# Bias rows of the last eleven groups kept in the transposed x: two heads stored at once, the rest two units later

## Chip, cores and metric

The kernel runs on one core of a Trainium2 chip. The metric is the device time of one execution in microseconds, the median of three runs. The profile is of one further execution of the same program.

## What is computed

Attention with a position bias that is computed on the way, followed by a gated feed-forward layer. Shapes: q, k, v are 4 x 8 x 576 x 64 (batch, heads, positions, width), the feed-forward weights 512 x 2048 and 2048 x 512.

```
psi  = log1p(|i - j|) / log1p(max(i, 1))          # 576 x 576, the same for all batches
bias = relu(psi * w1 + b1) @ w2                   # hidden 32, one value per head
attn = softmax(q k^T / 8 + bias) @ v
x    = attn with the heads side by side           # 2304 x 512
h    = x @ w_in
out  = (h * cos(h)) @ w_out
```

## The kernel before

Everything is float32; matmuls of the attention and the feed-forward layer use operands split in a high and a low float32r half. Work is put on the engines in the order in which the program issues it, and waits follow from reads and writes of the same bytes.

**First stage, the bias.** The 576 query positions are 36 groups of 16, put in five tiles: tile 4 has four groups, tiles 0 to 3 eight each. They are made in the order of `todo`: tile 4, then 0, 1, 2, 3. For a group DVE (one step in six: ACT) makes the hidden values `ht`, PE multiplies them with w2 into PSUM (`pa`, L356), and `bias_store` (L366) copies the 591 columns that the 16 positions share, scaled by the position's factor, into a buffer `rt` (L374, once on DVE, L372) and issues one store to `sc`, a DRAM tensor per tile (L375). Partition 8r + h of `rt` is head h of row r, so one store carries all eight heads: 128 rows. `ra` has eight `rt` buffers.

**Loads of the bias.** `load_bias(hp, t, heads)` (L267) reads the rows of tile t for the two heads of pair hp back from `sc` into `bt` tiles, each row shifted by one, so that every query position sees its own bias. For a head 0 that is one load, for a head 1 two (L273). The loads of the first pair are issued in the loop of the first stage, at steps n = 13 (tile 4), 20 and 21 (tile 0), 28 and 29 (tile 1), and after the last store (tiles 2 and 3). Those of later pairs follow in the last unit of the pair before.

**Attention.** There are 16 units (hp, b): four head pairs, and in each the four batches. A unit has five slots, one for each tile in the order 0, 1, 4, 2, 3; slot i is tile `tiles[i % 5]` of unit `i // 5`. In a slot PE makes the scores (`s`, L440) into two PSUM buffers, one for each head; DVE adds the bias and takes the maximum (L453); ACT takes the exponential (L471) and, on its other steps, copies turned blocks (`act_copy`, L529); GpSimd normalizes (L494). PE turns the result (L501) and multiplies with v (`pv`, L569) for slots that lie before. `keep_x` (L579) copies the product into `xT`, [128, 4, 2304]: its first quarter is written by units 0 to 3, the others by units 4 to 15.

**Loads in the slots.** Each slot ends with issues on SP's queue: v, k and q of later units (`load`, L153) and, in slots 5 and 6, the first two blocks of feed-forward weights (`load_w`, L77, tile `raw`). ACT reads the first of these in slot 9 (`abs_w`, L92), the second ten slots later. Loads, stores and bias loads all go through SP, which issues them in the program's order and stands while an instruction waits.

**Feed-forward.** It takes up the time behind some 280 us and runs on PE with both weight matrices.

Of the kernel before, what the change touches and what calls it, by code (L numbers as in the profile page):

```python
# [9 lines left out]
F32 = mybir.dt.float32  # L10
# [18 lines left out]
def kernel(  # L29
# [11 lines left out]
    nc = tc.nc  # L41
# [6 lines left out]
    RB = S + 15  # L48
    PITCH = S + 32
    GP = 16 * (8 * PITCH - 1)  # L50
# [15 lines left out]
    xT = const.tile([128, HP, NT], F32, name="xT")  # L66
    xs = const.tile([128, 2, KD, TB], F32R, name="xs")
    wpre = [const.tile([128, 2, 2, 512], F32R, name=f"wpre{i}") for i in range(WPRE)]
    sc = [dram.tile([1, (8 if t < 4 else 4) * GP + 16], F32, name=f"sc{t}") for t in range(5)]
# [7 lines left out]
    def load_w(fc, part):  # L77
        r = wk.tile([128, 512, 2], U32, tag="raw", name="raw")
        if part == 0:
            nc.sync.dma_start(  # L80
                out=r.rearrange("p (c x) y -> p c (x y)", c=KD),
                in_=w_in[:, fc * 256 : fc * 256 + 256].rearrange("(c p) x -> p c x", p=128),
            )
        else:
            nc.sync.dma_start(out=r.rearrange("p x y -> p (x y)"), in_=w_out[fc * 128 : fc * 128 + 128, :])
        raw[fc, part] = r
# [25 lines left out]
    with tc.manual_schedule():  # L112
        tail, front, stage = ExitStack(), ExitStack(), ExitStack()

        def opened(stack, name, bufs, side, space=None):
            kw = {} if space is None else {"space": space}
            return stack.enter_context(tc.tile_pool(name=name, bufs=bufs, side=side, reuse_waits="tile", **kw))
# [92 lines left out]
        def keep_hi(u, x, ps):  # L210
            for (hi, _), i, scale in halves_of(u, x, ps):
                nc.scalar.activation(out=hi, in_=i, func=AF.Copy, scale=scale)
# [8 lines left out]
        def bank(dt=F32):  # L221
            return ps_t.tile([128, 512], dt, tag="t", name="pt")
# [4 lines left out]
        def turn(u, x, ps):  # L227
            n = natural(u, x)
            for i, c in enumerate((4,) if x == "x" else range(4)):
                nc.tensor.transpose(ps[:, 128 * i : 128 * i + 128], n[:, c], ident)  # L230
            return ps
# [35 lines left out]
        def load_bias(hp, t, heads=range(2)):  # L267
            if t < 4:
                for h in heads:
                    bt = bp.tile([128, 576], F32, tag="b", name="bt")  # L270
                    src = sc[t]
                    for to, at, n in ((0, 0, S),) if h == 0 else ((0, 512, 64), (64, 0, 512)):
                        nc.sync.dma_start(  # L273
                            out=bt[:, to : to + n],
                            in_=bass.AP(
                                src.tensor,
                                src.offset + (2 * hp + h) * PITCH + 15 + at,
                                [[8 * PITCH - 1, 128], [1, n]],
                            ),
                        )  # L280
                    bias[hp, t, h] = bt
            else:
                bt = bp.tile([128, 576], F32, tag="b", name="bt")
                src = sc[t]
                for h in range(2):
                    nc.sync.dma_start(
                        out=bt[64 * h : 64 * h + 64],
                        in_=bass.AP(
                            src.tensor,
                            src.offset + (2 * hp + h) * PITCH + 15,  # L290
                            [[8 * PITCH - 1, 64], [1, S]],
                        ),
                    )
                bias[hp, t, 0] = bt

        ha = opened(stage, "ha", 10, "left")
        ra = opened(stage, "ra", 8, "left")
# [12 lines left out]
        wparts = [(fc, p) for fc in range(WPRE) for p in range(2)]  # L310
# [13 lines left out]
        for g in range(4):  # L324
            r = slice(32 * g, 32 * g + 32)
# [4 lines left out]
        def bias_hid(k):  # L330
            qi = groups[todo[k][0]][todo[k][1]]
            n = max(S - 16 * qi, 16 * qi + 16)
            hts = []
            for s in range(4):
                ht = ha.tile([128, S], F32, tag="h", name="ht")
                o = 4 * qi + s
                e = edge[:, o : o + 1]
                if s == 3 and k in ACT_H:
                    nc.scalar.activation(out=ht[:, 0:n], in_=wl[:, 0:n], func=AF.Relu, bias=e)  # L339
                else:  # L340
                    nc.vector.tensor_scalar(ht[:, 0:n], wl[:, 0:n], e, 0.0, ALU.add, ALU.max)  # L341
                hts.append(ht)
            return hts

        def bias_rows(k, hts):
            nr = 16 * groups[todo[k][0]][todo[k][1]] + 15
            ps = ps_a.tile([128, 1024], F32, tag="a", name="pa")
            at = 512 - nr if RB - 512 <= nr <= 512 else 0
            cuts = sorted({0, nr, 512 - at, RB})
            for a, b in zip(cuts, cuts[1:]):  # L350
                for s, ht in enumerate(hts):
                    if a < nr:
                        i = ht[:, nr - b + 1 : nr - a + 1][:, ::-1]
                    else:
                        i = ht[:, a - nr : b - nr]
                    nc.tensor.matmul(  # L356
                        ps[32 * s : 32 * s + 32, at + a : at + b],
                        nbd,
                        i,
                        start=True,  # L360
                        stop=True,
                        tile_position=(0, 32 * s),
                    )
            return ps[:, at : at + RB]

        def bias_store(k, ps):  # L366
            t, gi = todo[k]
            qi = groups[t][gi]
            rt = ra.tile([128, RB], F32, tag="r", name="rt")
            m = mrow[:, qi : qi + 1]  # L370
            if k == len(todo) - 2:
                nc.vector.tensor_scalar(rt, ps, m, None, ALU.mult)  # L372
            else:
                nc.scalar.activation(out=rt, in_=ps, func=AF.Copy, scale=m)  # L374
            nc.sync.dma_start(  # L375
                out=bass.AP(sc[t].tensor, sc[t].offset + gi * GP, [[PITCH, 128], [1, RB]]),
                in_=rt,
            )

        tiles = [0, 1, 4, 2, 3]  # L380
        for i in range(WPRE):
# [5 lines left out]
        todo = [(t, gi) for t in (4, 0, 1, 2, 3) for gi in range(len(groups[t]))]  # L387
        held, hts = None, bias_hid(0)
        nc.vector.tensor_copy(mrow, pm[:, 0:NQ])
        for n in range(len(todo) + 1):  # L390
            now = hts
            if n < len(todo):
                hts = bias_hid(n + 1) if n + 1 < len(todo) else None
                ps = bias_rows(n, now)
            if held:
                bias_store(*held)
            for t, heads in {13: ((4, ()),), 20: ((0, (0,)),), 21: ((0, (1,)),), 28: ((1, (0,)),), 29: ((1, (1,)),)}.get(n, ()):
                load_bias(0, t, heads)
            if n == len(todo):
                load_bias(0, 2)  # L400
                load(3, "k", (2, 3))
                load_bias(0, 3)
            held = (n, ps)
            if n in SECOND:
                load(2, *SECOND[n])
            if n in T_FIRST:
                halved[n] = turn(*T_FIRST[n], bank())
                keep_hi(*T_FIRST[n], halved[n])
            if n - 1 in T_FIRST:
                keep_lo(*T_FIRST[n - 1], halved[n - 1])  # L410
# [184 lines left out]
        W_MID = [(3, 9)]  # L595
        W_PLAN = [(0, 2), (0.5, 3), (1, 7), (2, 8), ("load", 8), (4, 12)]
        W_LATE = 10
        REST = {2: (1, 2), 3: (3, 4)}
        get = lambda i: jobs[i] if 0 <= i < len(jobs) else None

# [15 lines left out]
        def slot(i):  # L616
# [23 lines left out]
            else:  # L640
                if now:
                    qk(u, j)
                if last:
                    for h in heads_of(last):
                        softmax_exp(*last, h)
            weights(i - W_LATE, W_EARLY)
            if prev and prev[1] in (0, 2):
# [38 lines left out]
            if prev:  # L686
                keep_main(*prev, 0, pm[0])
            weights(i - W_LATE, W_MID)
            if j == 4 and u >= 1:
# [28 lines left out]
            if now:  # L718
                if i == 1:
                    load(0, "v")  # L720
                for du, x in LOAD_PLAN[j]:
                    if u + du < NU:
                        load(u + du, x, (0, 1) if (u, x) == (0, "k") else None)
                if i in (5, 6):
                    load_w(*wparts[i - 5])
                hp, b = units[u]
                if b == B - 1 and hp + 1 < HP:
                    load_bias(hp + 1, tiles[j])
                if i in X_EARLY:
                    split_x(0, 0, X_EARLY.index(i))  # L730
            weights(i - W_LATE, W_PLAN)
        for i in range(len(jobs)):
# [125 lines left out]
        def ffn_step(i, begun=False):  # L858
# [13 lines left out]
            if now:  # L872
                g, n, fc = now
                nx = steps[i + GF] if i + GF < len(steps) else None
                if nx:
                    for c in ((0, 1), (2, 3), (), ())[fc - g * GF]:
                        split_x(nx[0], nx[1], c)
                for step in REST.get(i, ()):
                    widen_w(*wparts[-1], step)
# [79 lines left out]
```

## Time and profile before

| | us |
|---|---|
| median of 3 runs | 695.43 |
| lowest and highest | 694.91, 697.91 |
| the profiled execution | 695.13 |
| its span, first to last instruction | 693.3 |
| PE busy | 679.7 (98%) |
| DVE busy | 580.8 (84%) |
| ACT busy | 435.8 (63%) |
| POOL busy | 398.2 (57%) |

PE, DVE, ACT and POOL are the engines for matmuls, for vectors, for activations, and GpSimd; PEld is PE's loading of weights, which runs beside its matmuls; SPq is the queue on which SP issues transfers. Times are from the start of the span. In the timeline an engine's idle time before an instruction stands in brackets, with what ended it. A line in the profile is a line of the kernel.

### The profile page before, as it was taken

To read this page: it belongs to the slowest core of one execution; us is meant where nothing else is said; L and a number is where in the kernel's file an instruction comes from. 1 tells how busy PE (TensorE), PEld (TensorE's weight loads), DVE (VectorE), ACT (ScalarE), POOL (GpSimd) and SP (SyncE) were. 2 spreads that over 40 slices of the span, in tenths; PEclk is the share of its full clock that TensorE was granted. 3 is DMA by queue.
4 is the path that set the end of the run, shared out by engine and by line. 5 is a ranking of instruction groups with operands and counts; after the bars stand their busy time and mean duration, and the time that the engine had idled before them with its cause. 6 is when DMAs were issued, how large, how long until landed. Compare 5 with 4: busy or idle time off the path is not lost.

```text
span 693.3 us, 15601 instructions
## 1 busy us (share of the span) xinstructions
PE 679.7 (98%) x5747; PEld 561.9 (81%) x5747; DVE 580.8 (84%) x1345; ACT 435.8 (63%) x938; POOL 398.2 (57%) x480
## 2 busy tenths in 40 slices
PE   6998999999999999999999999999999999999997
PEld 3666777777777777799989898998988888999986
DVE  8998888888888888678788789999899899876666
ACT  6998888988889887545565554454544544433342
POOL 0008888898988989646456356265374474463300
PEclk9999999999999999999999999999999999999999
DMA  6798546437337311012011111110111110011112
GB/s 161 266 350 224 130 122 168 104 85 220 71 92 200 99 50 41 10 31 61 30 34 60 30 49 44 32 61 32 34 58 31 57 35 32 0 46 46 47 46 92
DMA packets 84445, 58.57 MB, mean 84 GB/s; under 512 B 62224, under 2 KB 70800, under 8 KB 84368
## 3 DMA queue, kind: packets, MB, share of 16 engines
q1 hardware_dynamic: 83024, 56.88, 28.4%
q8 instruction: 46, 0.75, 0.5%
q10 hardware_dynamic: 1344, 0.69, 0.4%
q14 instruction: 31, 0.25, 0.1%
HBM read 41.94 MB, written 15.61 MB: 83 GB/s over the span
## 4 chain that ended last, share of the span: by engine, by line
PE 93%; DMA 3%; DVE 1%; POOL 1%; ACT 1%; issue 0%; SPq 0%; DVEq 0%; POOLq 0%
PE ph L759 29%; PE po L805 29%; PE pv L569 12%; PE s L440 11%; PE pm L501 6%; PE pa L356 4%; DMA sc<-rt 2%; PE pt L501 1%; PE spare L501 1%; DMA lt<-in_ltab_dram 1%; DMA bt<-sc 1%; POOL P L494 0%; DVE ht L341 0%; ACT ht L339 0%; DVE acc L829 0%
## 5 line engine op out<-in xcount | busy, mean ns | idle before, releaser
L453 DVE CUSTOM_DVE_ANT_0 P<-s,bt 128x576 f32<-128x576 f32 x144 | 103.8, 753 | 24.4 <-PE s L440 24.1
L494 POOL TENSOR_SCALAR P<-P,rc 128x576 f32<-128x576 f32 x144 | 108.3, 764 | 24.3 <-DVE rc L487 11.5
L763 ACT ACTIVATE a<-ph,quarter 128x384 int32<-128x384 f32 x96 | 55.7, 581 | 97.8 <-PE ph L759 96.9
L555 POOL TENSOR_TENSOR xs<-xT,xs 128x384 fp32r<-128x384 f32 x96 | 108.1, 1126 | 8.0
L471 ACT ACTIVATE P<-P,m 128x576 f32<-128x576 f32 x144 | 110.0, 768 | 0.6 <-DVE m L453 0.6
L759 PE MATMUL ph<-xs,wpre 128*128 128x384 f32 x576 | 109.4, 338 | 0.0
L759 PE MATMUL ph<-xs,w 128*128 128x384 f32 x576 | 108.5, 337 | 0.0
L774 ACT ACTIVATE r<-r,hpi 128x384 f32<-128x384 f32 x96 | 59.3, 617 | 74.8 <-DVE r L770 74.6
L759 PEld LDWEIGHTS ph<-xs,wpre 128*128 128x128 f32 x576 | 101.9, 188 | 5.4 <-DVE a L778 0.9
L759 PEld LDWEIGHTS ph<-xs,w 128*128 128x128 f32 x576 | 101.3, 188 | 5.1 <-DVE a L778 1.2
L769 DVE SCALAR_TENSOR_TENSOR r<-a,ph 128x384 f32<-128x384 int32 x96 | 52.8, 550 | 62.7 <-ACT a L763 62.6
L440 PE MATMUL s<-kN,qT 64*128 64x288 f32 (+1 forms) x864 | 92.0, 311 | 2.0 <-DVE m L453 1.4
L440 PEld LDWEIGHTS s<-kN,qT 64*128 64x128 f32 (+1 forms) x864 | 70.7, 185 | 27.2 <-DVE dn L484 7.6
L554 POOL TENSOR_SCALAR xs<-xT 128x384 fp32r<-128x384 f32 x96 | 63.2, 658 | 29.7 <-PE ph L759 29.7
L788 DVE TENSOR_TENSOR gl<-a,gh 128x384 fp32r<-128x384 f32 x96 | 75.8, 789 | 0.4 <-ACT gh L782 0.4
L569 PE MATMUL pv<-PT,vN 128*64 128x320 f32 (+1 forms) x512 | 76.0, 418 | 0.0
L805 PE MATMUL po<-wpre,gh 128*128 128x512 f32 x288 | 75.3, 397 | 0.0
L805 PE MATMUL po<-w,gh 128*128 128x512 f32 x288 | 75.2, 395 | 0.0
L110 POOL TENSOR_TENSOR w<-wb,w 128x512 fp32r<-128x512 f32 x16 | 20.8, 1297 | 87.6 <-ACT w L108 87.6
L782 ACT ACTIVATE gh<-a 128x384 fp32r<-128x384 f32 x96 | 49.8, 518 | 23.6 <-DVE a L778 23.6
L770 DVE SCALAR_TENSOR_TENSOR r<-a,r 128x384 f32<-128x384 int32 x96 | 61.0, 636 | 3.3
L805 PEld LDWEIGHTS po<-wpre,gh 128*128 128x128 f32 x288 | 53.4, 188 | 9.4 <-issue 0.5
(98 smaller groups left out, 1166.8 us busy)
## 6 DMA issues: line engine op xcount, KB each, us to landing
sc<-rt SPq DMA_DIRECT2D x36, 295.5 KB, 4.5
raw<-in_moe_w_in_dram SPq DMA_DIRECT2D x16, 512.0 KB, 3.7
raw<-in_moe_w_out_dram SPq DMA_DIRECT2D x16, 512.0 KB, 3.5
bt<-sc SPq DMA_DIRECT2D x16, 288.0 KB, 4.0
out_dram<-acc SPq DMA_DIRECT2D x17, 256.0 KB, 2.0
nk<-in_k_dram SPq DMA_DIRECT2D x32, 128.0 KB, 3.5
bt<-sc SPq DMA_DIRECT2D x16, 256.0 KB, 4.2
vN<-in_v_dram SPq DMA_DIRECT2D x32, 128.0 KB, 2.8
```

Of the source, the lines that this page charges most:

```text
L440: nc.tensor.matmul(s[h][:, hf, 0:HALF], qTs[u % 2][r, a, 128 * t : 128 * t + 128] if t < 4 else qTs[u % 2][:, a, 512:640], kN[u][r, b, o : ...
L453: nc.vector.tensor_tensor_reduce(neg.rearrange("p (a x) -> p a x", a=2), s[h][:, :, 0:HALF], bias[hp, t, h].rearrange("p (a x) -> p a x", ...
L471: nc.scalar.activation(out=P[u, j][:, 576 * h : 576 * h + 576], in_=neg, func=AF.Exp, bias=m[:, 0:1], scale=-1.0, accum_out=dn[u, j][:, h ...
L494: nc.gpsimd.tensor_scalar(p, p, r, 1.0, ALU.mult, ALU.mult)
L554: nc.gpsimd.tensor_scalar(h, src, 1.0, 1.0, ALU.mult, ALU.mult)
L555: nc.gpsimd.tensor_tensor(l, src, f(h), ALU.subtract)
L569: nc.tensor.matmul(ps[64 * h : 64 * h + 64, 0 : WQ[hf]], a, m, start=(c == 0), stop=(c == 4), tile_position=(0, 64 * h), skip_group_check= ...
L759: nc.tensor.matmul(ps, a, x, start=(i == 0), stop=(i == 3 * KD - 1))
L770: nc.vector.scalar_tensor_tensor(r, n, -TWO_PI_LO, r, ALU.mult, ALU.add)
L774: nc.scalar.activation(out=r, in_=r, func=AF.Sin, scale=SIN_SCALE, bias=hpi)
L788: nc.vector.tensor_tensor(gl, a, f(G[key][0]), ALU.subtract)
L805: nc.tensor.matmul(O[n][i], a[:, 128 * i : 128 * i + 128], w, start=(i0 == 0 and p == 0), stop=(i0 == GF - 1 and p == 2),)
```

## The change

The rows of the last eleven groups (three of tile 2, all of tile 3) are written into slices of `xT`, of which the last three quarters are free until unit 5 writes them, and no longer into a buffer of `ra`. At once only heads 0 and 1 of them are stored, with one store of 16 rows for each head. The full 128 rows are stored by `store_rows` in slots 6 to 14, and write heads 0 and 1 a second time with the same values. The bias of tile 2 for the first pair is loaded at steps n = 33 and 34 and no longer after the last store; there the two small loads of unit 3's k now come first and tile 3's bias follows. The first two weight blocks are loaded in slots 8 and 9 and no longer in slots 5 and 6.

```diff
+        rest = xT[:, 1:].rearrange("p h n -> p (h n)")
+        late = [rest[:, RB * i : RB * i + RB] for i in range(11)]
+
+        def store_rows(k, rt):
+            t, gi = todo[k]
+            nc.sync.dma_start(
+                out=bass.AP(sc[t].tensor, sc[t].offset + gi * GP, [[PITCH, 128], [1, RB]]),
+                in_=rt,
+            )
+
         def bias_store(k, ps):
             t, gi = todo[k]
             qi = groups[t][gi]
-            rt = ra.tile([128, RB], F32, tag="r", name="rt")
+            n = k - len(todo) + len(late)
+            rt = late[n] if n >= 0 else ra.tile([128, RB], F32, tag="r", name="rt")
             m = mrow[:, qi : qi + 1]
...
-            nc.sync.dma_start(
-                out=bass.AP(sc[t].tensor, sc[t].offset + gi * GP, [[PITCH, 128], [1, RB]]),
-                in_=rt,
-            )
+            if n < 0:
+                store_rows(k, rt)
+            else:
+                for h in range(2):
+                    nc.sync.dma_start(
+                        out=bass.AP(sc[t].tensor, sc[t].offset + gi * GP + h * PITCH, [[8 * PITCH, 16], [1, RB]]),
+                        in_=rt[h:128:8],
+                    )
...
-            for t, heads in {13: ((4, ()),), 20: ((0, (0,)),), 21: ((0, (1,)),), 28: ((1, (0,)),), 29: ((1, (1,)),)}.get(n, ()):
+            for t, heads in {13: ((4, ()),), 20: ((0, (0,)),), 21: ((0, (1,)),), 28: ((1, (0,)),), 29: ((1, (1,)),), 33: ((2, (0,)),), 34: ((2, (1,)),)}.get(n, ()):
                 load_bias(0, t, heads)
             if n == len(todo):
-                load_bias(0, 2)
                 load(3, "k", (2, 3))
                 load_bias(0, 3)
...
+        STORES = {6: (0, 1), 7: (2, 3), 10: (4, 5), 11: (6, 7), 12: (8,), 13: (9,), 14: (10,)}
...
-                if i in (5, 6):
-                    load_w(*wparts[i - 5])
+                if i in (8, 9):
+                    load_w(*wparts[i - 8])
+                for n in STORES.get(i, ()):
+                    store_rows(len(todo) - len(late) + n, late[n])
```

## Rows read from the trace of the kernel before

**Rows 1.** The page: busy time of PE and its share, instructions.
```profile
PE 679.7 (98%) x5747; PEld 561.9 (81%) x5747; DVE 580.8 (84%) x1345; ACT 435.8 (63%) x938; POOL 398.2 (57%) x480
```

**Rows 2.** Windows: length; busy PE, PEld, DVE, ACT, POOL; clock; DMA share; GB/s.
```profile
40.00:50.00 10.00, 10.00 (x153) 6.18 (x145) 9.88 (x27) 10.00 (x17) 0.00 (x0) 1.00 1.00 351
50.00:60.00 10.00, 8.41 (x101) 6.23 (x94) 6.87 (x21) 7.35 (x20) 5.69 (x8) 1.00 0.86 293
60.00:70.00 10.00, 8.86 (x121) 6.74 (x122) 8.65 (x33) 8.37 (x23) 9.71 (x14) 1.00 0.83 200
70.00:80.00 10.00, 10.00 (x136) 7.63 (x137) 7.67 (x26) 8.32 (x22) 8.82 (x13) 1.00 0.53 137
```

**Rows 3.** Waits from 36 to 75 us: total, times, longest.
```profile
PE s L440 <- DVE m L453: 1.4, 4, 0.7
...
DVE P L453 <- DMA bt<-sc: 0.3, 1, 0.3
```

**Rows 4.** Timeline around the first unit: start, length, instruction, idle time before.
```profile
51.21 0.76 ACT L374 ACTIVATE rt<-pa,mrow 128x591 f32<-128x591 f32 x1 [1.08 <-issue]
...
52.96 0.27 PE L230 MATMUL pt<-ident,nk 128*128 128x128 f32 x1
...
59.38 0.76 DVE L453 CUSTOM_DVE_ANT_0 P<-s,bt 128x576 f32<-128x576 f32 x1 [0.32 <-PE s L440]
...
61.87 0.76 DVE L453 CUSTOM_DVE_ANT_0 P<-s,bt 128x576 f32<-128x576 f32 x1 [0.31 <-PE s L440]
...
62.92 0.76 DVE L453 CUSTOM_DVE_ANT_0 P<-s,bt 128x576 f32<-128x576 f32 x1 [0.29 <-DMA bt<-sc]
...
63.75 1.05 PE L440 MATMUL s<-kN,qT 64*128 64x288 f32 x11 [0.66 <-DVE m L453]
```

**Rows 5.** The chain that ended last, from 36 to 75 us: start, length.
```profile
52.02 5.73 DMA sc<-rt
...
58.88 3.88 DMA bt<-sc
```

**Rows 6.** SP's queue: start, length, issues.
```profile
52.48 2.08 SPq L273 DMA_DIRECT2D bt<-sc  x3
...
57.82 1.50 SPq L273 DMA_DIRECT2D bt<-sc  x3
...
66.67 0.59 SPq L80 DMA_DIRECT2D raw<-in_moe_w_in_dram  x1
...
67.90 1.25 SPq L175 DMA_DIRECT2D nk<-in_k_dram  x2
...
70.53 1.73 SPq L175 DMA_DIRECT2D nq<-in_q_dram  x2
77.51 1.11 SPq L160 DMA_DIRECT2D vN<-in_v_dram  x2
```

**Rows 7.** Tile sc over the whole span: issue in ns, transfers from issue to landing.
```profile
L375 SPq DMA_DIRECT2D sc<-rt x36: 319/429/1752, 11.3 to 52.0; - x36
...
DMA to landing us min/median/max: 2.1/4.2/6.3
```

**Rows 8.** Tile raw from 60 to 130 us: issue to landing.
```profile
DMA to landing us min/median/max: 4.1/5.4/6.5
```

**Rows 9.** ACT's timeline in slot 9.
```profile
75.61 0.66 ACT L92 ACTIVATE wb<-raw 128x512 f32<-128x512 f32 x1
76.83 0.60 ACT L529 ACTIVATE PT<-pm 128x512 f32<-128x512 f32 x1 [0.56 <-PE pm L501]
78.09 0.44 ACT L529 ACTIVATE xT<-pv 128x320 f32<-128x320 f32 x1 [0.67 <-PE pv L569]
```

**Rows 10.** DVE by shape from 20 to 28 us: busy, mean ns.
```profile
L341 DVE TENSOR_SCALAR ht<-wl,edge 128x416 f32<-128x416 f32 x3 | 1.1, 428 | 0.0
```

**Rows 11.** The same from 36 to 44 us.
```profile
L341 DVE TENSOR_SCALAR ht<-wl,edge 128x416 f32<-128x416 f32 x4 | 1.5, 431 | 0.0
```

**Rows 12.** PE's timeline: the turn of the next k, slot 17.
```profile
97.83 0.41 PE L501 MATMUL spare<-ident,nk 64*128 64x64 f32 x8
```

## The prediction

> **What bounds the kernel now.** I read the engine totals first: PE is busy for nearly the whole span [rows 1]. What a change of loads and stores can win must therefore come out of PE's idle time. The windows say where that lies: PE loses 1.59 us between 50 and 60 us and 1.14 us between 60 and 70 us, 2.73 us together, and nothing in the stretch before or behind [rows 2]. The same rows show what tempts one to make this change: the DMA engines' share is 1.00 between 40 and 50 us, while the last bias rows are stored, and still 0.86 and 0.83 in the two windows after it.
>
> The second reading is who waits. Between 36 and 75 us one wait of a compute engine for a bias load is listed, 0.3 us long [rows 3]. The timeline shows it: DVE adds the second head of tile 3 at 62.92 us and has been idle for 0.29 us for that load; the first head of tile 3 and the first of tile 2 waited for PE's scores, not for a load [rows 4]. The chain names the transfers behind it: the last store of rows takes 5.73 us from its issue at 52.02 us, the load that waits for it leaves at 58.88 us and needs 3.88 us [rows 5]. So the store is on the chain that ended last, but only the last 0.29 us of it hold an engine up; the rest runs beside work that fills the time anyway. A share of the chain is not a saving.
>
> **The change part by part.** *Fewer bytes in the stores of groups 25 to 35.* A group is 128 rows of 591 floats, 302.6 kB; two heads of it are 32 rows, 75.6 kB. Eleven groups lose 11 x 227.0 = 2.50 MB, at the 351 GB/s of the window [rows 2] 7.1 us of DMA time before 52 us. The engines that make the rows do the same work into another buffer: PE, DVE and ACT have no idle time there to give back (10.00, 9.88 and 10.00 of 10 us, [rows 2]). Nor does the full DMA share lengthen their instructions: DVE's 416-column step takes 428 ns before the queue is full and 431 ns while it is [rows 10, 11]. This edit alone wins nothing; it only lets tile 3's rows land sooner.
>
> How much sooner: ACT writes the last group from 51.21 us for 0.76 us [rows 4], so its two stores leave at about 52.0 and 52.4 us (an issue takes 319 ns at least, 429 in the median, [rows 7]). Nearly idle, a transfer of this tensor lands in 2.1 us; in the full queue it takes up to 6.3 us [rows 7]. Both ends stay open. I take 2.1 to 3 us, since the eleven small stores bring a quarter of the bytes: landed at 54.5 to 55.4 us instead of 57.75. The loads of k that stand ahead of tile 3's bias in the queue need PE's turn at 52.96 us for 0.27 us [rows 4] and take about 1.25 us (two such issues, [rows 6]), so SP is free for the bias at 54.5 us at the earliest. Its three issues take 1.50 us [rows 6]; tile 3 leaves by 56.9 us and lands, with 3.9 us as before [rows 5], by 60.8 us, where DVE asks for it at 62.63 us (61.87 + 0.76, [rows 4]). Even at 5.73 us for the store it would be no later than before by more than one extra issue, 0.4 us.
>
> *What the vanished wait is worth.* DVE's second head starts at 62.63 instead of 62.92 us. PE stood for 0.66 us on the maximum that it gives [rows 4]; 0.37 us of that stay. Behind it PE is full from 70 us on [rows 2], so the 0.29 us can be carried to the end, if nothing there has less slack than PE. Bounds 0 and 0.29; I take 0.29.
>
> *Tile 2's bias loaded at steps 33 and 34.* Its issues go from 52.48 us, where they take 2.08 us of SP's time [rows 6], to some 3 us earlier. DVE needs tile 2 at 59.38 us and waits for PE there [rows 4]: worth nothing by itself, and it clears SP for tile 3, as counted. It puts a wait on SP for tile 2's last store, five groups back, and behind it queue the small stores of tile 3. These no longer hold a buffer of the ring of eight, so ACT doesn't wait for them.
>
> *Eleven full stores in slots 6 to 14.* They add 3.33 MB, 9.5 us of DMA time at 351 GB/s, from about 64 us on, where the share was 0.83 and then 0.53 [rows 2]. On SP each costs 0.32 to 0.66 us. Nobody waits for them until the second pair's bias loads. What they push back is the loads behind them. Those of slots 10 to 14 come behind the load of v at 77.51 us, which waits for PE [rows 6]; the next k and q are turned on PE only at 97.83 us [rows 12], so 2 to 3 us of extra issues before them are covered.
>
> *The first weight block, slot 8 instead of slot 5.* This is the edit that can cost. Before, it was issued at 66.67 us [rows 6] and ACT first reads it at 75.61 us [rows 9], with 4.1 us to landing at best and 6.5 at worst among the weight loads near [rows 8]: at least 2.4 us to spare. Now four full stores (1.3 to 2.6 us, 1.7 at the median issue), the k loads (67.90 to 70.53, 2.6 us) and the q loads (1.73 us) go ahead of it [rows 6, 7]: 6.0 us later, 72.7 us. Against that SP is past tile 3's bias at 56.4 us or so instead of 59.32 us (57.82 + 1.50, [rows 6]), 2.9 us sooner: 69.8 us. It lands between 73.9 and 76.3 us. ACT would ask 0.29 us sooner, at 75.3 us, so the middle has no wait. And ACT has 0.56 and 0.67 us of idle time in the same slot [rows 9], so a landing up to 76.5 us moves no copy that PE needs. I take 0.
>
> [...]
>
> Sum: 695.13 us of the profiled execution (693.3 of span, 1.83 around it) - 0.29 + 0 + 0 = 694.84 us. The median of the runs is 0.30 us above that execution: 695.1 us.
>
> **The rivals.** *The full queue was behind more of PE's idle time.* Then up to all 2.73 us come back: 692.7 us on the median. For it speaks that the gaps lie in the two windows with a DMA share of 0.86 and 0.83 [rows 2]; against it that only 0.3 us of waits name a load [rows 3], and that the heads before waited for scores [rows 4]. Those are the turns of two score buffers between PE and DVE, which no store touches. Chance 0.08.
>
> *The first weight block comes late (slower).* If SP wins nothing at tile 3 and the queue fills with the full stores, it is issued at 72.7 us and lands after 6.5 us at 79.2 us: 3.6 us after 75.61, less 1.23 us of ACT's slack, 2.4 us on PE: 697.5 us with the 0.29 us won. It decides from a landing at about 76.8 us on. For it: one slot between issue and use where there were four, and 605 kB of stores directly ahead of k and q; against it, 4.1 us is what a weight load took in a share of 0.83. With issues at 0.66 us and both mishaps it would reach 698.4 us. Chance 0.17.
>
> *The small stores cost as much of the queue as full ones (no change).* Then the last lands 5.73 us after an issue that comes one issue later; tile 3's wait stays and grows by up to 0.4 us: 695.4 to 695.9 us. For it: the count of stores in the stage doubles, and SP needed 0.43 us for each; against it, the two bounds of landing, 2.1 and 6.3 us [rows 7], differ with the load of the queue, and bytes fall to a quarter. Chance 0.13.
>
> **How the numbers follow.** The forecast has 0.62: 695.1 us, between 694.8 and 695.4 us by the bounds of its one term. The runs of before lie from 694.91 to 697.91 us, so half a per cent (3.5 us) is about what a measurement tells from no change. All four cases end inside it but for the tails. Range 693.0 to 697.6 us: it takes in the second rival's worked case and most of the first's. Faster by over 0.5% would take under 691.95 us, more than all of PE's idle time between 50 and 70 us: 0.03. Slower needs over 698.9 us, a weight block beyond 80 us or a wait not seen here: 0.06. Within: 0.91.
>
> **What would show it.** Right: the DMA share between 44 and 52 us well below 1, tile 3's bias issued near 55 us, no DVE wait for it, PE's wait near 63.5 us down to about 0.4 us, and everything behind earlier by some 0.3 us. The weight block issued near 70 us and ACT's first step on it with no idle time. Wrong: ACT idle for that block before about 75.3 us and PE idle soon after; a wait of the copies into the first quarter of xT (about 71, 78 and 85 us) for the stores that read its other quarters, if they are taken for one buffer; or PE's gaps between 52 and 62 us closing although no load was named in them.

## The result, and the profile after

The changed kernel takes 703.01 us (median of four runs, 701.71 to 704.88), the kernel before in the same comparison 695.54 us: ratio 1.0107, 95% interval 1.0091 to 1.0123. The forecast was 695.1 us with a range up to 697.6. The loss of 7.5 us is larger than any rival's.

The page of the changed kernel first. PE's busy time is 2 us longer than in [rows 1], the span 7.7 us.

```profile
PE 681.8 (97%) x5747; PEld 563.3 (80%) x5747; DVE 580.7 (83%) x1345; ACT 435.9 (62%) x938; POOL 396.7 (57%) x480
```

Its windows, columns as in [rows 2]. The DMA share between 40 and 50 us did fall, from 1.00 to 0.72. PE's busy time between 60 and 70 us fell too, from 8.86 to 4.00 us, and its clock column is 0.83 in two windows.

```profile
40.00:50.00 10.00, 10.00 (x152) 6.31 (x148) 10.00 (x29) 10.00 (x18) 0.00 (x0) 1.00 0.72 244
50.00:60.00 10.00, 8.46 (x98) 6.21 (x92) 6.89 (x22) 7.71 (x19) 4.91 (x7) 1.00 0.46 126
60.00:70.00 10.00, 4.00 (x56) 3.19 (x55) 4.56 (x15) 4.82 (x12) 5.42 (x8) 0.83 0.55 137
70.00:80.00 10.00, 10.00 (x125) 7.71 (x125) 7.20 (x26) 6.76 (x20) 7.57 (x10) 0.83 0.75 214
```

What VectorE (DVE) waited for, from its timeline in the changed kernel (start, length, idle time before and what ended it): three waits for bias loads, the second head of tile 2 and both of tile 3, 5.29 us together, where before there was one of 0.29 us [rows 4].

```profile
61.48 0.76 DVE L467 CUSTOM_DVE_ANT_0 P<-s,bt 128x576 f32<-128x576 f32 x1 [0.57 <-DMA bt<-sc]
...
66.71 0.76 DVE L467 CUSTOM_DVE_ANT_0 P<-s,bt 128x576 f32<-128x576 f32 x1 [3.73 <-DMA bt<-sc]
...
68.47 0.76 DVE L467 CUSTOM_DVE_ANT_0 P<-s,bt 128x576 f32<-128x576 f32 x1 [0.99 <-DMA bt<-sc]
```

And why the load was late: SP's queue in the changed kernel (start, length, issues). L390 is the store of one head, L273 the bias load. From 42.42 to 61.92 us SP issues 22 stores and six loads almost without a gap. Tile 3's bias leaves at 63.56 us, in the kernel before at 57.82 [rows 6].

```profile
42.42 4.40 SPq L390 DMA_DIRECT2D sc<-xT  x6
46.86 0.58 SPq L273 DMA_DIRECT2D bt<-sc  x1
47.54 1.73 SPq L390 DMA_DIRECT2D sc<-xT  x2
49.32 1.05 SPq L273 DMA_DIRECT2D bt<-sc  x2
50.47 4.91 SPq L390 DMA_DIRECT2D sc<-xT  x8
55.42 0.58 SPq L273 DMA_DIRECT2D bt<-sc  x1
56.10 1.10 SPq L390 DMA_DIRECT2D sc<-xT  x2
57.25 1.06 SPq L273 DMA_DIRECT2D bt<-sc  x2
58.41 3.51 SPq L390 DMA_DIRECT2D sc<-xT  x4
62.02 0.68 SPq L175 DMA_DIRECT2D nk<-in_q_dram  x1
62.74 0.64 SPq L175 DMA_DIRECT2D nk<-in_k_dram  x1
63.56 1.40 SPq L273 DMA_DIRECT2D bt<-sc  x3
```

ACT isn't what holds it up. It writes the first late group at 41.58 us and the last at 51.93 us, 0.72 us later than before [rows 4]. The last two stores leave only some 9 us after that. This is ACT's timeline:

```profile
41.58 0.81 ACT L385 ACTIVATE xT<-pa,mrow 128x591 f32<-128x591 f32 x1
...
51.93 0.76 ACT L385 ACTIVATE xT<-pa,mrow 128x591 f32<-128x591 f32 x1 [1.03 <-PE pa L356]
```

The view of the tensor sc in the changed kernel gives what one issue costs (min, median, max in ns). A store of 16 rows takes 587 ns of SP's time in the median, one of 128 rows out of the ring 406 ns: fewer rows don't make an issue shorter here.

```profile
L371 SPq DMA_DIRECT2D sc<-rt x25: 319/406/1534, 11.5 to 41.8; - x25
L390 SPq DMA_DIRECT2D sc<-xT x22: 472/587/1613, 42.4 to 61.3; - x22
```

So the rows of SP's queue add up: 15.65 us for the 22 stores, 3.27 us for the six loads and 0.58 us between the rows are 19.5 us, for eleven groups that ACT (for one of them DVE) writes in 11.1 us. Of the 15.65 us, 22 x 0.587 = 12.9 us are the stores at the median; the rest is gaps of SP and a few long issues, of which the first of the four at 58.41 us takes 1.61 us (the maximum in the row above). What makes these long isn't settled. A hint: beside this issue, between 56 and 60 us, and beside one of 1.10 us at 47.54 us, the transfers show one of 16 KB of the program's own instructions. The line from 56 to 60 us (packets, MB, share):

```profile
q8 instruction: 1, 0.02, 1.6%
```

The rest of the loss is put down to the clock. After the wait PE's granted clock is 0.50 until about 73.5 us, an estimate from the 0.65 between 72 and 74 us; windows of 2 us of the changed kernel show it:

```profile
64.00:66.00 2.00, 0.00 (x0) 0.00 (x0) 0.00 (x0) 0.53 (x1) 1.86 (x3) 1.00 0.71 170
66.00:68.00 2.00, 0.47 (x1) 0.28 (x1) 0.77 (x2) 0.49 (x1) 0.00 (x0) 0.65 0.99 252
68.00:70.00 2.00, 0.85 (x7) 0.71 (x8) 1.53 (x6) 1.11 (x4) 0.00 (x0) 0.50 0.66 148
70.00:72.00 2.00, 2.00 (x25) 1.88 (x25) 1.13 (x4) 0.47 (x4) 1.80 (x3) 0.50 0.95 214
72.00:74.00 2.00, 2.00 (x13) 1.01 (x15) 1.48 (x8) 1.95 (x8) 1.46 (x3) 0.65 0.69 205
74.00:76.00 2.00, 2.00 (x24) 1.22 (x20) 1.28 (x3) 0.85 (x3) 2.00 (x4) 1.00 0.92 272
```

PE's timeline of the changed kernel agrees: the eleven score matmuls behind the wait take 1.80 us, where [rows 4] has 1.05.

```profile
69.29 1.80 PE L454 MATMUL s<-kN,qT 64*128 64x288 f32 x11 [1.15 <-DVE m L467]
...
105.22 0.41 PE L515 MATMUL spare<-ident,nk 64*128 64x64 f32 x8
```

The last row is the turn of slot 17, at 97.83 us before [rows 12]: 7.39 us later. Of these 0.72 us were there at ACT's last group, from the first part of the stage, where nothing is changed (in the eleven profiled executions of the changed kernel and the experiments DVE's first score is taken between 52.2 and 53.4 us, in no order that goes with the edits); 5.29 - 0.29 = 5.00 us are DVE's waits; 1.67 us are left, and the lower clock is what the trace shows for them: the same 5747 matmuls keep PE busy for 2.1 us longer. This is a remainder and not a measurement of its own; the run with the wait filled, below, bears on it.

### The profile page after: what moved, and what is told of

It reads as the page before. It is cut to its first block, busy times and chain, and to the rows that moved or that the text cites. A ratio compares the mean times of both kernels' runs of the same rounds, so it can differ in the third digit from the quotient of the medians.

```text
span 701.0 us, 15611 instructions
## 1 busy us (share of the span) xinstructions
PE 681.8 (97%) x5747; PEld 563.3 (80%) x5747; DVE 580.7 (83%) x1345; ACT 435.9 (62%) x938; POOL 396.7 (57%) x480
## 4 chain that ended last, share of the span: by engine, by line
PE 93%; DVE 3%; DMA 1%; ACT 1%; SPq 1%; issue 1%; DVEq 0%; ACTq 0%
PE ph L776 29%; PE po L822 29%; PE pv L583 12%; PE s L454 11%; PE pm L515 6%; PE pa L356 4%; PE spare L515 1%; PE pt L515 1%; DVE ht L341 1%; DMA lt<-in_ltab_dram 1%; DVE P L467 1%; DMA bt<-sc 1%; SPq L390 0%; ACT ht L339 0%; ACT xT L385 0%
## 5 line engine op out<-in xcount | busy, mean ns | idle before, releaser
L822 PEld LDWEIGHTS po<-wpre,gh 128*128 128x128 f32 x288 | 53.4, 188 | 9.4 <-issue 0.5
```

What stands on the lines that cost most here:

```text
L822: nc.tensor.matmul(O[n][i], a[:, 128 * i : 128 * i + 128], w, start=(i0 == 0 and p == 0), stop=(i0 == GF - 1 and p == 2),)
```

## The experiments

Theory A: SP's queue can't issue two stores for each group in the time of a group, so the last rows leave late; bytes, order and the later stores don't matter. Theory B: the moved bias loads or the loads of k now ahead of tile 3's bias hold the queue. Theory C: the stores and weight blocks in the slots cost the time. Ratios are to the kernel before, with 95% intervals. Unless said, edits are to the changed kernel.

**One store for both heads.** The heads of a pair are put at places hp and hp + 4 of a row's eight (columns of w2 in another order), so that 32 rows, every fourth partition, hold the first pair.

```diff
-                for h in range(2):
-                    nc.sync.dma_start(
-                        out=bass.AP(sc[t].tensor, sc[t].offset + gi * GP + h * PITCH, [[8 * PITCH, 16], [1, RB]]),
-                        in_=rt[h:128:8],
-                    )
+                nc.sync.dma_start(
+                    out=bass.AP(sc[t].tensor, sc[t].offset + gi * GP, [[4 * PITCH, 32], [1, RB]]),
+                    in_=rt[0:128:4],
+                )
...
-                                src.offset + (2 * hp + h) * PITCH + 15 + at,
+                                src.offset + (hp + 4 * h) * PITCH + 15 + at,
```

> The changed kernel, but the two heads of a pair stand at places hp and hp + 4 of a row's eight, so that the first pair leaves in one store of 32 rows instead of two stores of 16; the full stores in slots 6 to 14, the moved bias loads and the moved weight blocks stay. Theory A (SP's queue can't issue 22 stores and 6 loads in the time of eleven groups: about 0.6 us for each in a row): with 11 issues less, the last store leaves near 53 us instead of 61.3 us, tile 3's bias near 55 us instead of 63.6 us, no engine waits for it, TensorE's clock stays at its upper level, and the time is that of the kernel before or 0.3 us less, 695 us (ratio to before 0.998 to 1.002). Theory B (the bias load of tile 2 ahead of the last stores, or the loads of k ahead of tile 3's bias, hold the queue): still about 703 us. Theory C (the full stores and weight blocks in the slots cost the time): still 700 us or more.

Measured: 695.87 us, ratio 0.9996 (0.9981 to 1.0011). The loss is gone with the count of stores; everything else of the change is in this kernel, so B and C fall. SP's queue shows it: the last two stores leave from 52.56 us, tile 3's bias at 56.01 us.

```profile
52.56 1.09 SPq L389 DMA_DIRECT2D sc<-xT  x2
...
56.01 1.27 SPq L273 DMA_DIRECT2D bt<-sc  x3
```

DVE takes tile 3's second head without a wait, and in the list of waits from 36 to 90 us of this kernel one DMA is left, the weight block:

```profile
ACT wb L92 <- DMA raw<-in_moe_w_in_dram: 1.6, 1, 1.6
```

**Full stores at once.** The late groups go whole out of the transposed x, with no stores in the slots.

```diff
-                for h in range(2):
...
+                store_rows(k, rt)
...
+        STORES = {}
```

> The changed kernel with the eleven late groups stored whole and at once, one store of 128 rows each out of the transposed x, and no stores in the slots; the moved loads stay. Theory A: 11 issues as in the kernel before, so no lateness of several us; 695 to 696 us, with the DMA share near 1 between 40 and 50 us as before. Theory B (the moved loads): about 703 us. Theory C (stores in the slots): about 695 us as well, so this run doesn't part A from C, the run with one store does.

Measured: 698.32 us (695.14 to 699.51), ratio 1.0031 (1.0017 to 1.0046), 2 us over what was expected; the kernel before lies between 694.68 and 700.04 us beside it. The profiled execution, at 695.14 us the fastest of the ten, has no wait of DVE for a bias load. What the others waited for was not profiled; with all bytes in the queue tile 3's bias leaves at 57.80 us, as late as before, so little lateness is spare. That the 7.5 us are not in the moved loads is shown, since these are in this kernel; the 2 us over the expectation stay open.

**Second head from GpSimd's queue.**

```diff
-                    nc.sync.dma_start(
+                    (nc.gpsimd if h else nc.sync).dma_start(
```

> The changed kernel with the store of the second head issued from GpSimd's queue, which has no work in this stage; count, bytes and rows of all transfers stay. Theory A: SP has 11 issues less, tile 3's bias leaves near 55 us and the time is 695 to 696 us. If it is the 22 transfers themselves that are too many for the DMA engines, or that their landing holds the later ones back: 701 us or more, whoever issues them.

Measured: 696.14 us, ratio 1.0005 (0.9992 to 1.0019). The same 22 transfers, half of them issued elsewhere, cost nothing: it isn't the DMA engines that are short, it is SP's time. One part was missed: tile 3's bias leaves at 57.31 us and not near 55, 1.74 us after the end of the issue ahead of it in SP's queue (55.57 us). What SP waits for there was not shown; DVE still takes it without a wait.

**The loads in their old order.**

```diff
-  33: ((2, (0,)),), 34: ((2, (1,)),)
...
+                load_bias(0, 2)
                 load(3, "k", (2, 3))
                 load_bias(0, 3)
```

> The changed kernel with tile 2's bias loaded behind the last store again, ahead of the loads of k, as in the kernel before. Theory A: SP is as late as with the change, the last store leaves some 1.7 us sooner (three loads less ahead of it, near 59.6 us) but tile 2's bias now leaves after it, near 60 us, where VectorE asks for it at 60.2 us: VectorE waits some 3 to 4 us for tile 2 and 1 to 2 us more for tile 3; 701 to 705 us. Theory B (the moved loads are the cause): 695 to 696 us.

Measured: 703.64 us, ratio 1.0114 (1.0099 to 1.0130), as A has it. SP issues fourteen stores in a row in 9.24 us, tile 2's bias leaves at 61.18 us, and DVE waits 5.34 and 0.48 us for its two heads, more than the 3 to 4 expected, and only 0.18 us for tile 3, where 1 to 2 were expected. From SP's queue, then DVE's timeline:

```profile
51.89 9.24 SPq L390 DMA_DIRECT2D sc<-xT  x14
61.18 1.53 SPq L273 DMA_DIRECT2D bt<-sc  x3
```

```profile
64.57 0.76 DVE L468 CUSTOM_DVE_ANT_0 P<-s,bt 128x576 f32<-128x576 f32 x1 [5.34 <-DMA bt<-sc]
```

**Two whole halves.** Two stores of 64 neighbouring partitions at once, none later.

```diff
+                        out=bass.AP(sc[t].tensor, sc[t].offset + gi * GP + 64 * h * PITCH, [[PITCH, 64], [1, RB]]),
+                        in_=rt[64 * h : 64 * h + 64],
...
+        STORES = {}
```

> The changed kernel with each late group stored whole and at once in two stores of 64 rows, neighbouring partitions, and no stores in the slots: 22 issues as in the change, but no row left for later and no step of eight partitions. Theory A (the number of issues): SP is as late as with the change or later, the last store leaves at 60 us or later and lands slower, since the DMA engines move all bytes; 702 to 706 us. If it is the form of the small stores (16 rows, a step of eight partitions) that makes an issue slow: each issue near 0.43 us, the last store before 57 us, 695 to 698 us.

Measured: 704.24 us, ratio 1.0129 (1.0114 to 1.0144). The form of the small stores is not the cause: an issue of 64 neighbouring rows takes 588 ns in the median, that of 16 rows with a step 587. From the view of sc of this kernel:

```profile
L390 SPq DMA_DIRECT2D sc<-xT x22: 445/588/1839, 42.2 to 61.6; - x22
```

**Eleven issues that move nothing of use.** Behind each store of the kernel with one store of 32 rows a second one of 1 kB to a tensor that nobody reads.

```diff
+                nc.sync.dma_start(out=extra[0:1, 256 * n : 256 * n + 256].rearrange("o (p x) -> (o p) x", p=16), in_=rt[0:16, 0:16])
```

> The kernel with one store of 32 rows, and behind each of the eleven a second store on SP that nobody reads: 16 rows of 64 bytes to a tensor of its own, 1 kB. Bytes, order and all other transfers are those of the run with one store (ratio 0.9996). Theory A (the number of issues on SP's queue alone): the last store of bias rows leaves at 58 to 61 us in place of 53.1, VectorE waits 2.5 to 5 us for tile 3 and the time is 699 to 703 us. If bytes or the form of the bias stores made the lateness: 696 us.

Measured: 702.60 us, ratio 1.0106 (1.0091 to 1.0121): the whole loss is back, with 11 kB. In SP's queue of this kernel the pace is plain. A pair of stores takes 1.17 us, ACT 1.01 us for a group (11.1 us for eleven), so whatever the loads between them cost is never made up:

```profile
51.60 0.45 SPq L390 DMA_DIRECT2D sc<-xT  x1
52.10 0.58 SPq L395 DMA_DIRECT2D extra<-xT  x1
52.77 0.45 SPq L390 DMA_DIRECT2D sc<-xT  x1
53.27 0.58 SPq L395 DMA_DIRECT2D extra<-xT  x1
```

**Five groups, and five idle issues.** First the change with the last five groups alone; then the idle store behind the last five of the kernel with one store.

```diff
-        late = [rest[:, RB * i : RB * i + RB] for i in range(11)]
+        late = [rest[:, RB * i : RB * i + RB] for i in range(5)]
```

> The changed kernel with only the last five groups kept and stored in two parts; the six before them go whole through the ring of buffers as in the kernel before; three slots hold their full stores. Theory A: 5 issues more than before in place of 11, at about 0.6 us each some 3 us of lateness, less what SP had to spare; last store near 57 us, tile 3's bias near 59 us, VectorE waits 0 to 1.5 us; 695.5 to 697.5 us, so that the loss isn't in proportion to the count but begins where SP's spare time ends. If every two-part store costs its share: 703 less 6/11 of 7.5, 699 us.

> The same with the idle store behind the last five groups alone. 5 issues at about 0.6 us make 3 us; SP was 3.0 us early with one store (tile 3's bias at 56.0 us, landed some 2 us before it was asked for). Theory A with spare time on SP: tile 3's bias leaves by 59 us, VectorE waits 0 to 0.5 us, 695.5 to 696.5 us; then the 2.5 us of waits with five two-part groups came from issues made longer by the full DMA queue, not from the count of five alone. If five issues are enough by themselves: 699 us or more.

Measured: 700.71 us, ratio 1.0076 (1.0059 to 1.0093), and 697.14 us, ratio 1.0022 (1.0011 to 1.0033). Both miss what A expected, the first by 3 us, the second by 0.6. With five two-part groups behind six whole ones, the first four small stores stretch over 3.99 us, and this isn't the length of their issues alone: SP's list of waits names landings of earlier transfers for 1.6 us ahead of small stores. With the DMA queue still full of whole stores (a share of 1.01 between 40 and 50 us) SP is held up by landings too, and the count of issues doesn't give the time. DVE waits 1.60 and 0.88 us for tile 3. With the idle issues, in an emptier queue (0.82), the one wait is 0.94 us. Rows of the first kernel's SP queue, of SP's waits in it (total, times, longest) and of the second's DVE timeline:

```profile
49.23 3.99 SPq L390 DMA_DIRECT2D sc<-xT  x4
```

```profile
SPq L390 <- DMA sc<-rt: 0.9, 3, 0.4
SPq L390 <- DMA bt<-sc: 0.7, 1, 0.7
```

```profile
63.68 0.76 DVE L469 CUSTOM_DVE_ANT_0 P<-s,bt 128x576 f32<-128x576 f32 x1 [0.94 <-DMA bt<-sc]
```

What the expectation left out is the clock: in the profiled execution 0.94 us of wait became 1.31 us of idle PE, and the granted clock then fell. These are windows of the kernel with five idle issues:

```profile
64.00:66.00 2.00, 1.50 (x21) 1.50 (x22) 1.62 (x7) 1.05 (x4) 1.45 (x2) 0.78 0.79 179
66.00:68.00 2.00, 2.00 (x18) 1.23 (x14) 1.88 (x8) 1.58 (x6) 2.00 (x4) 0.50 0.97 214
```

**The wait filled.** Fourteen matmuls that nothing uses stand in slot 4, where PE waits for tile 3.

```diff
+            if i == 4:
+                fill = ps_v.tile([128, 512], F32, tag="v", name="fill")
+                for _ in range(14):
+                    nc.tensor.matmul(fill, qTs[0][:, 0, 0:128], kN[0][:, 0, 0:512], start=True, stop=True)
```

> The changed kernel with 14 matmuls of 128 x 512 that nothing uses, put on TensorE in slot 4, where it stands for 3.67 us and waits for tile 3's bias (14 take some 3.3 us at the upper clock). The wait for the bias stays as it is. If the lower clock behind the wait has a share of the loss: the granted clock stays 1.0 between 66 and 74 us, the eleven score matmuls behind the wait take 1.05 us in place of 1.80, and the time is 1.5 to 2 us less than with the change, 701 to 701.5 us. If the loss is all in the wait: 703 us.

Measured: 701.79 us, ratio 1.0092 (1.0077 to 1.0108). That is 1.2 us under the change, which the intervals of the two ratios don't part. The trace does: DVE's waits for bias add up to 5.36 us as before the filling, and slot 7's turn comes at 74.66 us, with the change at 76.61. But the clock did not stay at 1.0 as expected. It fell sooner, around 63.4 us, after PE had been idle for 1.08 us ahead of 62.26 us, was 0.50 between 64 and 66 us while PE did the filling (4.81 us in all, from 63.96 us), and was back at 1.00 when the useful work began:

```profile
62.00:64.00 2.00, 1.74 (x30) 1.62 (x30) 0.94 (x5) 0.87 (x2) 1.42 (x3) 0.85 0.16 40
64.00:66.00 2.00, 2.00 (x7) 1.61 (x6) 0.00 (x0) 0.60 (x1) 1.82 (x3) 0.50 0.74 185
66.00:68.00 2.00, 2.00 (x9) 1.58 (x8) 0.77 (x2) 0.72 (x2) 0.00 (x0) 0.79 0.99 254
68.00:70.00 2.00, 1.92 (x17) 1.30 (x17) 1.56 (x6) 0.99 (x4) 0.00 (x0) 1.00 0.66 149
```

Slot 17's turn is at 103.64 us here, 1.58 us sooner than with the change. DVE's first score is taken 0.19 us sooner too (52.83 us, with the change 53.02), so 1.39 us are left, with the waits as long as before. That fits a share of the clock of some 1.7 us; it is one execution of each kernel.

**One store, weight blocks in their old slots.**

```diff
-                if i in (8, 9):
-                    load_w(*wparts[i - 8])
+                if i in (5, 6):
+                    load_w(*wparts[i - 5])
```

> The kernel with one store of 32 rows for the first pair, with the two weight blocks loaded in slots 5 and 6 again, as before. There ScalarE waited 1.6 us for the first block in slot 9 and the stretch from the turns of slot 7 to those of slot 12 took 14.45 us, against 14.31 before. If the late block costs 0.14 us on TensorE: no wait of ScalarE, 14.31 us for the stretch, and 695.0 to 695.8 us, 0.1 to 0.2 us under the run with one store; the interval of the time can't tell that from nothing, the trace can.

Measured: 696.19 us, ratio 1.0007 (0.9998 to 1.0017). ACT's wait is gone, but the stretch from slot 7 to slot 12 stays at 14.46 us: the late block was not what it costs. PE's timeline of this kernel shows what is new. In slot 8 PE now waits 0.29 us for a copy by ACT, as much as the wait for tile 3 had been:

```profile
70.76 0.65 PE L514 MATMUL pm<-ident,P 64*128 64x64 f32 x14 [0.29 <-ACT PT L542]
```

## Why the prediction was wrong

**The step that failed** is the working of "how much sooner", "its two stores leave at about 52.0 and 52.4 us", and with it the bound that tile 3 would be "no later than before by more than one extra issue, 0.4 us". Both took SP as caught up with ACT; the last store left at 61.3 us, and tile 3's bias at 63.56 us where the prediction had it issued near 55. The extra issues ahead of that store were never added up. They were priced as bytes, and bytes fell; what grew was SP's own time. [rows 6] held the price of issues that follow each other: two in 1.25 us, three in 1.50 and in 2.08. 22 stores at 0.6 us and six loads at 0.5 us are 16 us, for a stretch of 11 us. Even at the 429 ns of [rows 7], which I took instead, the 28 issues are 12 us; and that is a median over 36 issues, of which 18 came after SP had waited for ACT's rows (14.9 us in all). The third rival named the doubled count and then charged one issue of it.

The second miss is the price of a wait. The rivals carry each us of wait to the end as one us. Here 5.0 us of waits came with another 1.7 us, put down to PE at the lower clock, and with five idle issues the clock fell behind a wait of 0.94 us.

**What held.** That the stores were on the chain for 0.29 us only: with one store the wait is gone and the time is the same. Of the 0.29 us about half reaches slot 17. With one store ACT's last group is at 51.36 us, 0.15 us later than before, and slot 17's turn at 97.82 us, 0.01 us sooner, so 0.16 us is left; the copy by ACT is next late in slot 8, the case that the prediction named ("less slack than PE"). In the measured time none of it can be told. That the later stores cost nothing: they are in the kernel with one store. The weight block did come late: ACT waited 1.15 us with the change and 1.6 us with one store, and the slack of 1.23 us that [rows 9] gave covered the first (from the turn of slot 7 to that of slot 12 PE needs 14.31 us with the change, as before). For all that, 703 us is not the second rival's 697.5: its mechanism was real and nearly free, its price lay elsewhere.

Theory A is shown by three runs that change one thing: fewer issues (0.9996), the same issues on another queue (1.0005), idle issues added (1.0106). Two issues of 0.59 us stand against a landing of 1.9 us here, and they repeat. The rows have 0.32 us for an issue at least and 0.43 to 0.59 us in a row.

Is it the issue itself or a limit on transfers in flight? With five two-part groups there is a sign of such a limit: SP waits there for landings, 1.6 us ahead of small stores. In the changed kernel SP's list of waits from 40 to 64 us names no landing, and the rows above with eleven idle issues leave 0.05 and 0.09 us between one issue and the next. The changed kernel's view of transfers from 44 to 56 us has 14 small stores with a median of 1.9 us to landing. So in these two kernels it is the issues. No run changed the number in flight by itself.

```profile
sc<-xT SPq DMA_DIRECT2D x14, 36.9 KB, 1.9
```

## What to carry to other kernels

A transfer split to move fewer bytes was paid for in issues here (0.59 us each): before splitting, add up what the issuing queue does per step (issues x 0.43 to 0.6 us, here) and hold it against the pace of the producer, the loads behind it included. Take the price of an issue from issues that follow each other, not from the median. If the queue is full, change the layout so that one store covers what is needed, or issue from an engine that is idle; here each of the two removed the loss, and neither beat the kernel before.

## What was not expected of the hardware

- An issue on SP's queue costs as much for 16 rows of 64 bytes (579 ns in the median, 11 of them) as for 16 rows of 2364 bytes (587 ns) or 64 rows (588 ns); size doesn't show in it. The stores of 32 rows ahead of those 1 kB ones take 453 ns in the median, less than these.
- A wait of 0.94 us on DVE, 1.31 us of idle time on PE, came ahead of a fall of the granted clock to 0.50; in the kernel before, whose longest gaps of PE between 50 and 70 us are 0.74 us (ahead of 55.53 us) and 0.66 us, it stayed at 1.00 [rows 2].
- The 27 runs of the kernel before beside the first experiments lie between 694.68 and 700.04 us, the 11 with one store between 695.47 and 696.47. Beside the later experiments 26 runs of the kernel before lie within 694.49 and 697.43 us. Whether fewer bytes ahead of tile 3's bias make the time steadier is open; no run was made to show that.
